# Attention and a gated expert layer on one core: pairs of column blocks in one bank for the first batch, and one head group's scores on four row strips

## The chip, the cores and the metric

The kernel runs on one core of one Trainium2 chip. The metric is the device time of one execution in microseconds, the median of several runs. Engines are named as in the profile: PE is TensorE (matmul), PEld its weight loads, DVE is VectorE, ACT is ScalarE, POOL is GpSimd, SP is SyncE. A lower time is better.

## The reference

Softmax attention over 8 batches of 12 heads, 448 tokens and 64 channels, and behind it a two-layer expert with a SiLU gate over all 3584 tokens.

```
scores = matmul(q, k^T) / 8;  attn = softmax(scores);  a = matmul(attn, v)
x = a with its heads side by side: 3584 x 768
h = x @ w_in            (768 x 2048)
g = h / (1 + exp(-h))
out = g @ w_out         (2048 x 768)
```

Inputs and the output are float32; the kernel computes in float16 with float32 sums.

## The kernel before

Work is cut into units of one batch and one head group (4 of the 12 heads). Batch 0 is cut in two pieces of 224 tokens (`PIECES`, line 211), so it has six units, 0 to 5; each later batch has three of 448 tokens. For a unit, `scores` (line 358) multiplies keys and queries. A head has 64 channels, held as two planes (`e`) of 32 rows, so a matmul uses one of four row strips of PE, one strip per head. The banks come in pairs: `y` = 0 holds heads 0 and 1, `y` = 1 heads 2 and 3, and there are two such pairs (`s_ring`). `expo` (line 378) takes the exponential of one pair of banks on ACT. `attend` (line 433) multiplies it, on four column strips, with ones (part 0, the sums) and with the values (parts 1 and 2). `inverse` (line 445) and `norm` (line 475) make x on DVE, and transposes on DVE (`turn_k`, `turn_q`) prepare keys and queries.

In `qk_seq` (lines 1289 to 1294) a unit below `HALVES` = 6, that is, every unit of batch 0, issues its scores in halves: one burst for `y` = 0 and one for `y` = 1, each on two row strips and each needing one free pair of banks. A unit from `HALVES` on issues one burst on all four strips and needs both pairs.

The first expert matmul, `ffn1` (line 503), goes by column blocks `f` of 128 of the 2048 columns, six matmuls each over the 768 rows. For batch 0 each of the two pieces has its own 16 blocks of 224 tokens; a bank holds 512 numbers per partition, and every block takes a bank of its own (tag `m`, four banks, shared with the attend tiles and the results of the second matmul). `tanh` (line 516) makes tanh(h) on ACT, with three buffers, and `gate` (line 547) computes (tanh(h) + 1) h on DVE, into `G`; x was made half as large, which turns this into the SiLU. The gate gives the bank back. `plain` (line 717) is the second matmul for the first four token tiles of batch 0, and `product` (line 701) for the later ones.

The order of every engine is laid down when the kernel is built. A planner (`Order`, line 82, and the loop at line 1473) keeps a clock for each engine with assumed durations, picks what PE does next among scores, attend tiles and expert work, and lets ACT and DVE take ready operations by their bias. What it emits is each engine's program; on the chip an engine runs it in order and waits at semaphores. So a small change of a duration or a ring moves many later instructions. Until the first block of `ffn1`, PE fills gaps with matmuls on zeros (`run_zeros`, line 1464), which hold one of the four `m` banks. The loads are issued by POOL in a fixed order; the results are stored from SP.

Names in the profile: `s` scores, `E` exponentials, `a` attend tiles, `xT` x, `h` first matmul, `th` Tanh, `G` gates, `o` and `p` second matmul, `T` sums of exponentials, `z` the zeros.

Of the kernel before, what the change touches and what calls it, by code (L numbers as in the profile page):

```python
# [9 lines left out]
FP16 = mybir.dt.float16  # L10
FP32 = mybir.dt.float32
AF = mybir.ActivationFunctionType
ALU = mybir.AluOpType
# [12 lines left out]
def mm(n):  # L26
    return n / 2400.0 + 0.0026


def act(n):  # L30
    return n * 0.00087 + 0.13
# [138 lines left out]
def kernel(  # L170
# [9 lines left out]
    nc = tc.nc  # L180
# [20 lines left out]
    LONES = (0, 1, 2, 3)  # L201
    NPL = 4
    EAGER = 1
    HALVES = 6
    NEAR, LATE = 0.15, -2.0
    COLD, FIRST = 8.5, 47
    SHY = 0.5
# [11 lines left out]
    sb = ctx.enter_context(tc.tile_pool(name="sb", bufs=1))  # L219
    ps = ctx.enter_context(tc.tile_pool(name="ps", bufs=1, space=bass.MemoryType.PSUM))  # L220
# [134 lines left out]
    def per_burst(n):  # L355
        return 2 if units[n][0] == 0 else 1
# [111 lines left out]
    def x3(b, cc):  # L468
        if (b, cc // 3) not in xT:
            xT[(b, cc // 3)] = sb.tile(  # L470
                [128, 3, S], FP16, name=f"xT_{b}_{cc // 3}", tag="xT", bufs=NX3
            )
        return xT[(b, cc // 3)]
# [15 lines left out]
    def times(out, w, x, start, stop, strips):  # L489
        cut = 32 if strips else 128  # L490
        for i in range(0, 128, cut):
            nc.tensor.matmul(  # L492
                out=out[i : i + cut],
                lhsT=w[:, i : i + cut],
                rhs=x,
                start=start,
                stop=stop,
                skip_group_check=True,
            )

    h_t, th_t, o_t = {}, {}, {}

    def ffn1(b, f, t0, t1, strips):
        h = ps.tile([128, 512], FP32, name=f"h_{b}_{f}_{t0}", tag="m", bufs=4)
        for cc in range(NDC):
            times(
                h[:, 0 : t1 - t0],
                w_in_t[:, cc, 128 * f : 128 * (f + 1)],
                x3(b, cc)[:, cc % 3, t0:t1],
                cc == 0,  # L510
                cc == NDC - 1,
                strips,
            )
        h_t[(b, f, t0)] = h

    def tanh(b, f, t0, t1):
        th = sb.tile([128, t1 - t0], FP16, name=f"th_{b}_{f}_{t0}", tag="th", bufs=3)
        nc.scalar.activation(out=th, in_=h_t[(b, f, t0)][:, 0 : t1 - t0], func=AF.Tanh)  # L518
        th_t[(b, f, t0)] = th


# [4 lines left out]
    G = const.tile([128, NFF, 2 * S], FP16, name="G")  # L526
# [20 lines left out]
    def gate(b, f, t0, t1):  # L547
        r = b % 2
        cut = 6 * 128 - S if b % 4 == 1 else S
        for lo, hi, dst, at in ((0, cut, G, S * r), (cut, S, X, -cut)):  # L550
            lo, hi = max(lo, t0), min(hi, t1)
            if lo < hi:
                nc.vector.scalar_tensor_tensor(  # L553
                    out=dst[:, f, at + lo : at + hi],
                    in0=th_t[(b, f, t0)][:, lo - t0 : hi - t0],
                    scalar=1.0,
                    in1=h_t[(b, f, t0)][:, lo - t0 : hi - t0],
                    op0=ALU.add,
                    op1=ALU.mult,
                )  # L560
# [223 lines left out]
    od = Order(SHY)  # L784
    s_ring, m_ring, e_ring = Ring(2), Ring(4), Ring(NE)
# [3 lines left out]
    kt_op, qt_op, exp_op, rdn_op, x_op, g_op = {}, {}, {}, {}, {}, {}  # L789
# [54 lines left out]
    for n in range(NB0 + NG, NU):  # L844
        b, hg = units[n][:2]
# [40 lines left out]
    moe = []  # L886
    x_left = {}
    ffn1_left = {b: 0 for b in range(B)}
# [5 lines left out]
    quads, gates_of = [], {}  # L894

    def queue_ffn1(b, g0, g1):
        t0, t1 = 32 * g0, 32 * g1
        for f in range(NFF) if b == 0 else [x for f in range(HF) for x in (f, f + HF)]:

            def run(f=f):  # L900
                strips = b > 0 and od.mode == "cols" and bool(qk_seq or av_seq)
                op = Op("PE", NDC * mm(t1 - t0), lambda: ffn1(b, f, t0, t1, strips), tail=PE_OUT)
                if warm["on"]:
                    warm["on"] = False
                    m_ring.give(od.now)
                m_ring.take()
                od.on_pe(op, "cols" if strips else "full")
                th = od.add(
                    Op("ACT", act(t1 - t0), lambda: tanh(b, f, t0, t1), [op], -3 if b == 0 else -0.3, tail=0.2)
                )  # L910
                g = Op(
                    "DVE",
                    (t1 - t0) / 960.0 + 0.13,
                    lambda: gate(b, f, t0, t1),
                    [th],
                    -4,
                    then=m_ring.give,
                )
                g_op.setdefault((b, f), []).append(od.add(g))
                ffn1_left[b] -= 1  # L920

            def deps(f=f):
                made = [(x_op[(b, cc, g0)], cc * mm(t1 - t0)) for cc in range(NDC)] + ld_win[f]

                u, r = divmod(b, 2)
                for qd in range(NT * B // 4) if u else ():
                    if any(t // NT == u - 1 and (r or t % NT < 4) for t in (2 * qd, 2 * qd + 1)):
                        made += (
                            [plain_op.get(x) for x in ((0, 0), (0, 1), (1, 0), (1, 1))]
                            if qd == 0  # L930
                            else [pr_op.get((qd, m)) for m in (1, 2, 3, 4, 7)]
                        )
                return made

            moe.append((deps, 1, run, ()))
            ffn1_left[b] += 1

    pair_w, pair_x = {}, {}
# [297 lines left out]
    def after_x(n):  # L1236

        b, hg, g0, g1 = units[n]
        x_left[(b, g0)] = x_left.get((b, g0), NG) - 1
        if x_left[(b, g0)]:  # L1240
            return
        if b == PB:
            return
        if b > PB:
            for qd in range(1, NT * B // 4):
                if max(batches(qd)) >= PB:
                    queue_quad(qd)
            return
        queue_ffn1(b, g0, g1)
        if g1 < TPP:  # L1250
            return
        if b == 0:
            sums_w((5, 6, 4))
            for j in range(2):
                for t in range(2):
                    queue_plain(t, j)
        for qd in range(1, NT * B // 4):
            if max(batches(qd)) == b:
                queue_quad(qd)
# [28 lines left out]
    for ns in jobs:  # L1288
        if len(ns) == 1:
            split = ((0,), (1,)) if ns[0] < HALVES else ((0, 1),)  # L1290
            qk_seq += [(ns, c, ys) for c in range(NCH // per_burst(ns[0])) for ys in split]
        else:
            split = ((0,), (1,)) if ns[0] < HALVES else ((0, 1),)
            qk_seq += [([n], c, ys) for n in ns for c in range(NCH - 1) for ys in split]
# [178 lines left out]
    while True:  # L1473
# [44 lines left out]
        if warm["on"] and od.free["PE"] <= od.now and wait > 0.06 and od.now > 0.9:  # L1518
            each = mm(128) if od.now > COLD else 0.107
            n = max(1, int((wait - 0.06) / each), int(wait / each + 0.9) * (od.now < COLD))  # L1520
            if warm.pop("first", None):
                n = FIRST
# [36 lines left out]
```

## Time and profile before

| What | Value |
|---|---|
| Median of three runs | 392.9 us (392.55 to 393.38) |
| The profiled execution's own time | 392.49 us |
| Its span in the profile | 390.7 us |
| Granted clock of PE | 90% of full speed or more in each of 40 slices |
| Tanh, 224 wide (batch 0) | 32 of 363 ns |
| Tanh, 448 wide | 80 of 545 ns |
| Gate, 224 wide (batch 0) | 32 of 382 ns |
| Gate, 448 wide | 48 of 616 ns |
| Exponential, 128 x 896 | 156 of 915 ns |
| Add of exponentials on DVE | 40 of 1084 ns |
| Block of `ffn1`, 6 matmuls of 224, ahead of another one | 0.575 us on PE |

The times come from the profiled execution. A busy time of PE is modelled at its ends, since matmuls overlap in the pipe: what a group costs PE is read as the distance from its start to the start of the next group. In a line of the timeline the columns are start, duration, engine, line of the kernel, operation, output and input, the tile's shape and the count; a bracket gives the engine's idle time before it and what ended that. "issue" means that the profile shows nothing that was waited for.

### The profile page before, as it was taken

The numbers are of one execution on the slowest core, as the hardware profiler recorded it, in microseconds if no ns is written. First come the engines' busy times: TensorE is split into PE (matmuls) and PEld (weight loads), VectorE is DVE, ScalarE is ACT, GpSimd is POOL, SyncE is SP. The second block draws the span as 40 slices with busy tenths as digits, with TensorE's granted clock in tenths as the row PEclk, the third lists the DMA queues.
The fourth block names the chain that finished last, engine by engine and source line by source line (L and its number), as shares of the span: only waits on it lengthen the run. The fifth ranks groups of instructions, "written<-read, shape, count | busy, mean of one in ns | idle before, by whom it ended". The sixth has DMA issues, their size and how long they took to land.

```text
span 390.7 us, 10672 instructions
## 1 busy us (share of the span) xinstructions
PE 384.3 (98%) x4369; PEld 206.3 (53%) x4369; DVE 274.6 (70%) x570; ACT 253.7 (65%) x399; POOL 89.1 (23%) x173
## 2 busy tenths in 40 slices
PE   8999999999999999999999999999999999999995
PEld 7667774444454444545445444544445655556663
DVE  2466676999996877987588758666869984447441
ACT  4988885697766779666774676466783238882220
POOL 7632365415006243400643014000000000000000
PEclk9999999999999999999999999999999999999999
DMA  7999999929039582814956139002100131001333
GB/s 114 202 210 210 159 161 190 187 42 139 1 62 151 121 105 40 119 47 89 145 82 88 40 73 168 7 0 59 27 0 3 42 93 29 0 3 41 92 95 98
DMA packets 35361, 34.52 MB, mean 88 GB/s; under 512 B 11376, under 2 KB 33776, under 8 KB 35312
## 3 DMA queue, kind: packets, MB, share of 16 engines
q0 software_dynamic: 24784, 22.82, 39.5%
q1 hardware_dynamic: 9952, 10.33, 9.8%
q8 instruction: 34, 0.56, 0.6%
q10 hardware_dynamic: 576, 0.69, 0.6%
q14 instruction: 15, 0.12, 0.1%
HBM read 45.61 MB, written 11.01 MB: 145 GB/s over the span
## 4 chain that ended last, share of the span: by engine, by line
PE 97%; DMA 1%; ACT 1%; issue 0%; POOL 0%; DVE 0%; POOLq 0%
PE p L492 31%; PE h L492 29%; PE s L346 13%; PE a L409 11%; PE f L492 8%; PE o L492 3%; PE a L425 2%; DMA rq<-in_q_dram 1%; PE z L1468 1%; ACT E L383 1%; POOL rk L255 0%; ACT ost L768 0%; DVE rq L333 0%; ACT th L518 0%; POOLq L1543 0%
## 5 line engine op out<-in xcount | busy, mean ns | idle before, releaser
L383 ACT ACTIVATE E<-s 128x896 f16<-128x896 f32 (+1 forms) x172 | 149.8, 915 | 38.0 <-PE s L346 36.5
L492 PE MATMUL h<-xT,w_in_t 128*32 128x448 f16 (+2 forms) x1086 | 117.2, 336 | 0.0
L492 PEld LDWEIGHTS <-w_in_t 128*128 128x128 f16 (+1 forms) x1158 | 71.2, 97 | 56.3 <-issue 11.5
L518 ACT ACTIVATE th<-h 128x448 f16<-128x448 f32 (+1 forms) x112 | 54.2, 493 | 36.8 <-PE h L492 31.1
L553 DVE SCALAR_TENSOR_TENSOR G<-th,h 128x448 f16<-128x448 f16 (+2 forms) x112 | 55.7, 509 | 23.4 <-ACT th L518 21.7
L492 PEld LDWEIGHTS <-G 128*128 128x128 f16 (+1 forms) x580 | 43.1, 98 | 32.4 <-issue 4.6
L768 ACT COPY ost<-p 128x384 f32<-128x384 f32 x52 | 24.9, 480 | 53.5 <-PE p L492 47.1
L346 PE MATMUL s<-rq,KT 32*128 32x448 f16 (+4 forms) x768 | 51.0, 337 | 0.8 <-ACT E L383 0.4
L280 POOL DMA_DIRECT2D V<-in_v_dram x88 | 48.3, 559 | 14.2 <-DMA w_out_t<-in_moe_w_out_dram 6.8
L492 PE MATMUL p<-w_out_t,G 128*128 128x384 f16 (+1 forms) x352 | 49.5, 326 | 0.0
L409 PE MATMUL a<-E,V 128*32 128x448 f16 (+2 forms) x864 | 42.3, 333 | 0.0
L492 PEld LDWEIGHTS <-S 128*128 128x128 f16 (+1 forms) x408 | 30.0, 98 | 22.7 <-issue 2.3
L261 POOL DMA_DIRECT2D rq<-in_q_dram x27 | 15.1, 558 | 102.6 <-PE s L346 79.0
L492 PE MATMUL p<-D,S 128*128 128x384 f16 (+1 forms) x256 | 37.2, 326 | 0.0
L774 DVE TENSOR_TENSOR ost<-p,ost 128x384 f32<-128x384 f32 x39 | 21.6, 554 | 18.7 <-PE p L492 14.9
L480 DVE SCALAR_TENSOR_TENSOR xT<-a,rdn 128x448 f16<-128x448 f32 (+1 forms) x54 | 30.4, 569 | 5.8 <-PE a L409 3.6
L346 PEld LDWEIGHTS <-KT 32*128 32x128 f16 (+2 forms) x864 | 17.5, 98 | 29.1 <-issue 27.3
L409 PEld LDWEIGHTS <-V 128*32 128x32 f16 (+1 forms) x864 | 20.5, 96 | 18.8 <-issue 7.6
L394 DVE TENSOR_TENSOR T<-E,E 128x1792 f16<-128x1792 f16 x20 | 21.7, 1084 | 8.0 <-ACT E L383 8.0
L394 DVE TENSOR_TENSOR T<-T,E 128x1792 f16<-128x1792 f16 x20 | 21.7, 1083 | 5.7 <-ACT E L383 5.7
L315 DVE STREAM_TRANSPOSE KT<-rk 128x256 f32<-128x256 f32 (+3 forms) x48 | 16.6, 385 | 6.7 <-DMA rk<-in_k_dram 5.9
L492 PE MATMUL p<-w_out_t,S 128*128 128x384 f16 (+1 forms) x152 | 19.1, 326 | 0.0
(67 smaller groups left out, 321.1 us busy)
## 6 DMA issues: line engine op xcount, KB each, us to landing
out_dram<-ost SPq DMA_DIRECT2D x194, 48.0 KB, 1.6
rk<-in_k_dram POOLq DMA_DIRECT2D x24, 224.0 KB, 5.8
rq<-in_q_dram POOLq DMA_DIRECT2D x21, 224.0 KB, 5.7
w_in_t<-in_moe_w_in_dram POOLq DMA_DIRECT2D x6, 512.0 KB, 11.2
w_out_t<-in_moe_w_out_dram POOLq DMA_DIRECT2D x4, 768.0 KB, 13.5
V<-in_v_dram POOLq DMA_DIRECT2D x43, 64.0 KB, 3.7
V<-in_v_dram POOLq DMA_DIRECT2D x40, 48.0 KB, 4.0
out_dram<-ost SPq DMA_DIRECT2D x8, 96.0 KB, 2.1
```

The source lines that it names most:

```text
L280: nc.gpsimd.dma_start(out=VT[b][32 * x : 32 * (x + 1), hs, 0:count, :], in_=v[b, hs].rearrange("h (i g) d -> i h g d", g=TPP)[:, :, first ...
L315: nc.vector.transpose(out=pairs[:, x:y, 0:count], in_=t[:, first : first + count * (y - x)].rearrange("p (x c) i -> p x c i", c=count),)
L346: nc.tensor.matmul(out=pS[p0 : p0 + 32 * (x1 - x0), h % 2, at : at + nq], lhsT=KT[(b, hg)][32 * h : 32 * (h + 1), c, x0:x1, :, e], rhs=QT[ ...
L383: nc.scalar.activation(out=E[(n, w)][0:kr, 2 * y : 2 * y + 2, 0:nk], in_=pS_t[(n, w, y)][0:kr, :, 0:nk], func=AF.Exp, scale=attn_scale,)
L394: nc.vector.tensor_tensor(out=T[n], in0=T[n] if step else E[(n, 0)], in1=E[(n, step + 1)], op=ALU.add,)
L409: nc.tensor.matmul(out=a[32 * h : 32 * (h + 1), 0:nq], lhsT=w, rhs=e[k0:k1, h, at : at + nq], start=start, stop=stop,)
L480: nc.vector.scalar_tensor_tensor(out=x3(b, cc)[:, cc % 3, 32 * g0 : 32 * g1], in0=acc[(n, part)][:, 0:nq], scalar=0.5, in1=rdn_t[n].rearra ...
L492: nc.tensor.matmul(out=out[i : i + cut], lhsT=w[:, i : i + cut], rhs=x, start=start, stop=stop, skip_group_check=True,)
L518: nc.scalar.activation(out=th, in_=h_t[(b, f, t0)][:, 0 : t1 - t0], func=AF.Tanh)
L553: nc.vector.scalar_tensor_tensor(out=dst[:, f, at + lo : at + hi], in0=th_t[(b, f, t0)][:, lo - t0 : hi - t0], scalar=1.0, in1=h_t[(b, f, ...
L768: nc.scalar.copy(out=ost(qd, *OUT[m]), in_=bank(qd, BANK[m]))
L774: nc.vector.tensor_tensor(out=t, in0=bank(qd, BANK[m]), in1=t, op=ALU.add)
```

## The change

Three edits, and what the planner makes of them.

First, batch 0's blocks of the first matmul go in pairs. `blocks(b)` is 2 for batch 0 and 1 for the others. Block `f` even opens a bank, block `f` + 1 writes the next 224 columns of the same bank. One Tanh and one gate of 448 serve both, the gate with a three-dimensional access that spreads the two blocks over `G`. The planner takes one bank for a pair, and Tanh and gate depend on the pair's second block. In batch 0 there are then 16 Tanh and 16 gates in place of 32 each.

Second, the wait of an odd block is tied to the even one before it, which has to have been issued (`parts`).

Third, `HALVES` is 5 in place of 6. Unit 5, the last head group of batch 0, issues its scores in two bursts of 16 matmuls on all four row strips in place of four bursts of 8.

```diff
-    HALVES = 6
+    HALVES = 5
...
     def ffn1(b, f, t0, t1, strips):
-        h = ps.tile([128, 512], FP32, name=f"h_{b}_{f}_{t0}", tag="m", bufs=4)
+        i = f % blocks(b)
+        if i == 0:
+            h_t[(b, f, t0)] = ps.tile(
+                [128, 512], FP32, name=f"h_{b}_{f}_{t0}", tag="m", bufs=4
+            )
+        h = h_t[(b, f - i, t0)]
         for cc in range(NDC):
             times(
-                h[:, 0 : t1 - t0],
+                h[:, (t1 - t0) * i : (t1 - t0) * (i + 1)],
...
+    def blocks(b):
+        return 2 if b == 0 else 1
+
     def tanh(b, f, t0, t1):
-        th = sb.tile([128, t1 - t0], FP16, name=f"th_{b}_{f}_{t0}", tag="th", bufs=3)
-        nc.scalar.activation(out=th, in_=h_t[(b, f, t0)][:, 0 : t1 - t0], func=AF.Tanh)
+        n = (t1 - t0) * blocks(b)
+        th = sb.tile([128, n], FP16, name=f"th_{b}_{f}_{t0}", tag="th", bufs=3)
+        nc.scalar.activation(out=th, in_=h_t[(b, f, t0)][:, 0:n], func=AF.Tanh)
...
-            if lo < hi:
+            if b == 0 and lo < hi:
+                nc.vector.scalar_tensor_tensor(
+                    out=G[:, f : f + 2, t0:t1],
+                    in0=th_t[(b, f, t0)].rearrange("p (f t) -> p f t", f=2),
+                    scalar=1.0,
+                    in1=h_t[(b, f, t0)][:, 0 : 2 * (t1 - t0)].rearrange("p (f t) -> p f t", f=2),
+                    op0=ALU.add,
+                    op1=ALU.mult,
+                )
+            elif lo < hi:
...
-                m_ring.take()
+                n = blocks(b)
+                if f % n == 0:
+                    m_ring.take()
                 od.on_pe(op, "cols" if strips else "full")
+                ffn1_left[b] -= 1
+                if f % n < n - 1:
+                    parts.append(f)
+                    return
...
             def deps(f=f):
+                if f % blocks(b) and f - 1 not in parts:
+                    return [None]
```

The built order of PE in the new kernel, from unit 3's sums on, where it leaves the old one: unit 3's attend (all three groups), unit 5's first burst, unit 4's sums, one zeros matmul, unit 4's attend, the first block of `ffn1`, unit 5's second burst, five more blocks, unit 6's first scores, unit 5's attend. The old order: unit 3's sums, one zeros matmul, then unit 5's four half bursts, each followed by one attend group (the last by two), the first block, unit 6's first scores, unit 5's attend. Behind that the two orders differ in detail until the second block of batch 4 and are then the same to the end. The work itself is the same, but that four matmuls of the second layer in batch 0 no longer run as four column strips each (12 instructions fewer).

More of the change, by code (lines that the diff above doesn't have):

```diff
@@ L513, in ffn1 @@
             )
-        h_t[(b, f, t0)] = h
+    def blocks(b):
+        return 2 if b == 0 else 1
     def tanh(b, f, t0, t1):
-        th = sb.tile([128, t1 - t0], FP16, name=f"th_{b}_{f}_{t0}", tag="th", bufs=3)
-        nc.scalar.activation(out=th, in_=h_t[(b, f, t0)][:, 0 : t1 - t0], func=AF.Tanh)
+        n = (t1 - t0) * blocks(b)
+        th = sb.tile([128, n], FP16, name=f"th_{b}_{f}_{t0}", tag="th", bufs=3)
+        nc.scalar.activation(out=th, in_=h_t[(b, f, t0)][:, 0:n], func=AF.Tanh)
         th_t[(b, f, t0)] = th
@@ L896, in queue_ffn1 @@
     def queue_ffn1(b, g0, g1):
-        t0, t1 = 32 * g0, 32 * g1
+        t0, t1, parts = 32 * g0, 32 * g1, []
         for f in range(NFF) if b == 0 else [x for f in range(HF) for x in (f, f + HF)]:
@@ L905, in run @@
                     m_ring.give(od.now)
-                m_ring.take()
+                n = blocks(b)
+                if f % n == 0:
+                    m_ring.take()
                 od.on_pe(op, "cols" if strips else "full")
+                ffn1_left[b] -= 1
+                if f % n < n - 1:
+                    parts.append(f)
+                    return
+                f0, nq = f - n + 1, n * (t1 - t0)
                 th = od.add(
-                    Op("ACT", act(t1 - t0), lambda: tanh(b, f, t0, t1), [op], -3 if b == 0 else -0.3, tail=0.2)
+                    Op("ACT", act(nq), lambda: tanh(b, f0, t0, t1), [op], -3 if b == 0 else -0.3, tail=0.2)
                 )
@@ L912, in run @@
                     "DVE",
-                    (t1 - t0) / 960.0 + 0.13,
-                    lambda: gate(b, f, t0, t1),
+                    nq / 960.0 + 0.13,
+                    lambda: gate(b, f0, t0, t1),
                     [th],
@@ L918, in run @@
                 )
-                g_op.setdefault((b, f), []).append(od.add(g))
-                ffn1_left[b] -= 1
+                od.add(g)
+                for i in range(f0, f + 1):
+                    g_op.setdefault((b, i), []).append(g)
             def deps(f=f):
+                if f % blocks(b) and f - 1 not in parts:
+                    return [None]
                 made = [(x_op[(b, cc, g0)], cc * mm(t1 - t0)) for cc in range(NDC)] + ld_win[f]
@@ L933, in deps @@
                 return made
-            moe.append((deps, 1, run, ()))
+            moe.append((deps, int(f % blocks(b) == 0), run, ()))
             ffn1_left[b] += 1
```

## The prediction

> **What bounds the kernel now.** I read the page first, for the engines and the chain, then the timeline of PE where the order of work changes, then the transfers of narrow windows. The page:
>
> ```profile
> PE 384.3 (98%) x4369; PEld 206.3 (53%) x4369; DVE 274.6 (70%) x570; ACT 253.7 (65%) x399; POOL 89.1 (23%) x173
> ...
> q8 instruction: 34, 0.56, 0.6%
> ...
> PE 97%; DMA 1%; ACT 1%; issue 0%; POOL 0%; DVE 0%; POOLq 0%
> ```
>
> PE is busy for 98% of the span and is 97% of the chain, so an edit counts only by what it does to PE: work taken off it, changes of tiling mode, or stalls. ACT and DVE have slack on the average (65% and 70%). The second line is the queue that fetches instructions: 0.56 MB in 34 packets is 16.5 KB each, and PE's 8738 instructions over 34 are 257 per packet. I come back to it. PE's timeline, the start and the stretch in which the order changes:
>
> ```profile
> 5.97 0.60 PE L346 MATMUL s<-rq,KT 32*128 32x224 f16 x16 [0.33 <-DVE rq L333]
> 6.50 0.62 PE L1468 MATMUL z<-zeros 128*128 128x128 f16 x8
> ...
> 24.11 0.57 PE L409 MATMUL a<-E,ones 128*32 128x224 f16 x16
> 24.61 0.23 PE L1468 MATMUL z<-zeros 128*128 128x128 f16 x1
> 24.78 0.57 PE L346 MATMUL s<-rq,KT 32*128 32x224 f16 x8
> 25.28 0.57 PE L409 MATMUL a<-E,V 128*32 128x224 f16 x16
> 25.78 0.57 PE L346 MATMUL s<-rq,KT 32*128 32x224 f16 x8
> 26.28 0.57 PE L409 MATMUL a<-E,V 128*32 128x224 f16 x16
> 26.78 0.60 PE L346 MATMUL s<-rq,KT 32*96 32x224 f16 x8
> 27.31 0.56 PE L409 MATMUL a<-E,ones 128*32 128x224 f16 x13
> 28.13 0.28 PE L409 MATMUL a<-E,ones 96*32 96x224 f16 x3 [0.26 <-issue]
> 28.34 0.60 PE L346 MATMUL s<-rq,KT 32*96 32x224 f16 x8
> 28.87 0.96 PE L409 MATMUL a<-E,V 128*32 128x224 f16 x32
> 29.76 0.75 PE L492 MATMUL h<-xT,w_in_t 128*128 128x224 f16 x6
> ```
>
> The price of a group is the distance between two starts. PE runs in a fixed order without holes except one: the group at 27.31 stops after 13 of its 16 matmuls and goes on at 28.13. It took 1.03 where its like at 25.28 took 0.50, and the profile names no semaphore for the 0.53. The other hole after 10 us is here:
>
> ```profile
> 50.85 1.27 DVE L553 SCALAR_TENSOR_TENSOR G<-th,h 128x224 f16<-128x224 f16 x4
> 51.28 1.70 PE L409 MATMUL a<-E,V 128*32 128x448 f16 x32
> 51.58 1.72 ACT L383 ACTIVATE E<-s 128x896 f16<-128x896 f32 x2
> 52.91 1.00 PE L346 MATMUL s<-rq,KT 32*128 32x448 f16 x8
> 53.85 3.05 PE L492 MATMUL h<-xT,w_in_t 128*128 128x224 f16 x30
> ```
>
> The gates came late behind an add of 1.05 us on DVE at 49.88. So the attend group got its bank 0.08 us late (51.28), one Tanh waited for its buffer, the two exponentials behind it ended at 53.30, and the scores at 52.91, which need both of their banks, took 0.94 instead of 0.51.
>
> **The change part by part.** PE's order is the same in both kernels up to the group at 24.11 and again from the second block of batch 4 (241.4 us) to the end. So the sum is made over what lies between.
>
> *Scores of unit 5.* Four bursts of 8 matmuls on two row strips become two of 16 on four. Now: 0.50 + 0.50 + 0.53 + 0.53 = 2.06 us (24.78 to 25.28, 25.78 to 26.28, 26.78 to 27.31, 28.34 to 28.87). No row has the interleaved form. Upper end: strips do not overlap, 2.06 again. Lower end: as many columns per strip as the 448-wide burst at 30.44, which ends at 30.94: 0.50, and 0.53 with 96 rows, 1.03. Nearest is the kernel's first burst, 16 matmuls from 5.97 to 6.50, 0.53 with its strips one pair behind the other; with 0.03 for 96 rows I take 0.53 + 0.56 = 1.09. Gain 0.97.
>
> *Mode changes.* Two attend groups in a row take 0.89 (28.87 to 29.76), 0.40 and 0.49, against 0.50 ahead of scores. In the new order the first two of unit 3 stand ahead of another attend group: 0.2 saved. The second burst of unit 5 now stands between two blocks of the first matmul, which costs one more change, 0.1. Gain 0.1.
>
> *Pairs in a bank.* 32 Tanh of 363 ns become 16 of 545 (the 448-wide row), 32 gates of 382 ns become 16 of 616: 11.6 to 8.7 us on ACT and 12.2 to 9.9 on DVE, both under PE, so nothing by itself. PE's matmuls are the same. What it can cost is that a bank is held from the first block's start to the pair's gate. A pair takes 2 x 0.575 on PE, and Tanh and gate behind it some 1.4 with hops; four banks last 4.6 us. Following each bank by its rows to the first block of batch 1, I find every one free 0.4 us or more before PE asks. Bounds for what is not followed behind that: 0 to 0.5 us lost; I take 0, because PE had no hole over 0.1 us from 54 to 380 us with such work.
>
> *The wait at 52.91.* In the new order a block of the first matmul (0.67) stands between the attend groups and these scores, and the Tanh three pairs on waits for a gate that is done before the add on DVE starts. PE comes 2.8 us behind the previous burst, its exponentials end some 2.5 behind it. Gain 0.08 + 0.43 = 0.51; bounds 0 and 0.51.
>
> *Moved steps.* The full burst waits for both exponentials of unit 4 (end 25.14; PE comes at 25.41) and the second one for both of unit 5's first (end about 28.0); behind them stand attend groups and first blocks. The first block of the first matmul goes ahead of the second burst; its weights have landed by 23.0 us, the second half's by 33.9 (first used at about 36.6), the last quarter of w_out by 61.2 (used at about 65). The turn of the next keys moves behind unit 4's norms, ending near 30.8; its scores come at 33.1. POOL's and SP's queues keep their order.
>
> *The hole at 28.13.* Windows of the transfers show one fetch packet at 19.6, 25.7 and 31.7 each, six microseconds apart in the stretch where q0 keeps the engines over 100% busy, the middle one being
>
> ```profile
> q8 instruction: 1, 0.02, 5.1%
> ```
>
> between 25.6 and 26.7, and none from 26.7 to 31.6. PE passes some 257 instructions in the same six microseconds. My reading: PE came to the end of a block and the next, landed at 26.6, was usable 1.5 us later. At the other two boundaries PE comes 1.5 to 1.6 us behind the landing too. The block holds the same instructions by number in the new kernel: 86 matmuls after 24.11, which is now the sixth of unit 4's second attend group. PE gets there at 24.11 + 0.40 + 0.40 + 0.50 + 0.53 + 0.49 + 0.16 + 0.10 = 26.69. The packet was asked for before 24.11, so it comes at the same time: PE stands until 28.13, 1.44 us instead of 0.53. Loss 0.91. The next block would be usable near 34.1, and PE asks for it at about 34.6. Bounds: gain 0.53 (no hole) to loss 0.91.
>
> [...]
>
> Sum: -0.97 - 0.10 - 0.51 + 0.91 = -0.67 us. The profiled execution took 392.49 us around its span of 390.7, 0.4 under the median of 392.9; the span goes to 390.0 and the median to 392.2.
>
> **Rivals.** *The hole is no block boundary.* Then it is gone or as short as before: -0.97 - 0.10 - 0.51 - 0.53 = -2.11, 390.8 us. For it: PE passes the boundaries before and behind with no hole. Against: it stands where packet and count put it. [...]
>
> *Banks held too long (slower).* Where attend tiles of 0.87 us take one of the four banks, three are left, 3.45 us. A pair whose Tanh finds an exponential ahead (0.92) and whose gate finds an add (1.08) holds its bank for 1.15 + 0.2 + 0.92 + 0.55 + 1.08 + 0.62 = 4.5 us. PE then stands about 1 us, and the place comes at three points in batch 0 (unit 5's attend, unit 6's sums, unit 6's attend). It decides once two of them meet both: 392.2 + 2 = 394.2. For it: DVE's add did this once before, at 49.88. Against: two Tanh and two gates less stand in each queue, and the order puts the add elsewhere.
>
> *The burst gains nothing.* If strips interleave no better than in turn, 0.97 stays: 393.2. Against it the row at 5.97.
>
> **How the numbers follow.** Forecast 62%, no-boundary 18%, held banks 12%, burst without gain 8%. What a measurement can tell from no change is about 0.2%, 0.79 us. The forecast's gain of 0.67 lies just under it; with 0.4 us of doubt on the unfollowed stretch and the runs (their spread is 0.8) it is faster in 25, the same in 36, slower in 1 of its 62. No-boundary is faster; the burst case splits 1, 6, 1; held banks slower. Faster 0.44, the same 0.42, slower 0.14. The range 390.5 to 393.4 holds the first two and the burst case, and leaves out mainly held banks.
>
> **What would show it.** In the new profile: two bursts of 16 at about 25.4 and 29.6, each near 0.55; a hole in unit 4's second attend group that ends near 28.1, with a fetch packet near 25.7; no hole at unit 8's first scores; Tanh near 545 and gates near 616 ns, 16 each; the second block of batch 4 at about 240.7. Wrong would be: no hole at 26.7 (the first rival), PE waiting for G in batch 0 (the second), bursts near 1 us (the third), or new holes from 75 to 240 us.

## The result and the profile after

| | Before | After |
|---|---|---|
| Median, side by side | 392.74 us (392.12 to 393.38, 10 runs) | 391.52 us (391.33 to 392.24, 10 runs) |
| Ratio | | 0.9973, 95% interval 0.9965 to 0.9981 |
| The profiled execution | 392.49 us, span 390.7 | 391.46 us, span 389.7 |

The change is worth 1.2 us in these medians and 1.0 us in the two spans; the forecast was 0.67. A second set of runs gave 391.85 beside 392.51 us, a ratio of 0.9981 (0.9972 to 0.9990): 0.7 us. So the runs alone give the gain no closer than 0.7 to 1.2 us. The page of the kernel after: the engines, PE's share of the chain, and the groups of Tanh and of gates.

```profile
PE 382.6 (98%) x4357; PEld 205.2 (53%) x4357; DVE 273.7 (70%) x554; ACT 251.9 (65%) x383; POOL 89.1 (23%) x173
...
PE 97%; DMA 1%; issue 0%; ACT 0%; POOL 0%; DVE 0%; POOLq 0%
...
L526 ACT ACTIVATE th<-h 128x448 f16<-128x448 f32 x96 | 52.4, 546 | 33.5 <-PE h L492 27.8
```

PE still sets the end. The Tanh have one width left, 546 ns, and 1.8 us of ACT and 0.9 us of DVE went without PE's share changing. The gates by shape show the 16 new ones at 618 ns beside the old 448-wide ones at 616:

```profile
L570 DVE SCALAR_TENSOR_TENSOR G<-th,h 128x448 f16<-128x448 f16 x48 | 29.1, 616 | 14.7 <-ACT th L526 13.8
L561 DVE SCALAR_TENSOR_TENSOR G<-th,h 128x448 f16<-128x448 f16 x16 | 9.9, 618 | 8.1 <-ACT th L526 8.1
```

PE's timeline of the kernel after where the order changed, and at unit 8's first scores:

```profile
24.17 0.57 PE L409 MATMUL a<-E,ones 128*32 128x224 f16 x16
24.56 0.95 PE L409 MATMUL a<-E,V 128*32 128x224 f16 x32
25.44 0.58 PE L346 MATMUL s<-rq,KT 32*128 32x224 f16 x16
25.95 0.57 PE L409 MATMUL a<-E,ones 128*32 128x224 f16 x16
26.45 0.23 PE L1495 MATMUL z<-zeros 128*128 128x128 f16 x1
26.61 0.36 PE L409 MATMUL a<-E,V 128*32 128x224 f16 x5
27.84 0.86 PE L409 MATMUL a<-E,V 128*32 128x224 f16 x27 [0.86 <-issue]
28.63 0.75 PE L492 MATMUL h<-xT,w_in_t 128*128 128x224 f16 x6
29.31 0.61 PE L346 MATMUL s<-rq,KT 32*96 32x224 f16 x16
29.85 3.05 PE L492 MATMUL h<-xT,w_in_t 128*128 128x224 f16 x30
...
51.86 1.71 PE L409 MATMUL a<-E,V 128*32 128x448 f16 x32
53.49 0.75 PE L492 MATMUL h<-xT,w_in_t 128*128 128x224 f16 x6
54.18 0.57 PE L346 MATMUL s<-rq,KT 32*128 32x448 f16 x8
54.68 1.51 PE L492 MATMUL h<-xT,w_in_t 128*128 128x224 f16 x14
```

Read by starts: the two bursts of unit 5 take 0.51 (25.44 to 25.95) and 0.54 (29.31 to 29.85). The hole stands in unit 4's second attend group: five matmuls, then nothing until 27.84, with no semaphore named. The two groups take 2.02 us (26.61 to 28.63) against 0.89 for the pair ahead of the same block in the kernel before (28.87 to 29.76), so PE stood 1.13 us; before, it stood 0.53 (a group of 1.03 for one of 0.50). Unit 8's first scores take 0.50 in place of 0.94.

Where the time went, added up over all starts of PE from unit 3's sums to the second block of batch 4:

```
               before   after   difference
scores          34.78   33.22   -1.56
attend          37.26   37.65   +0.39
first matmul    77.30   77.40   +0.10
second matmul   67.74   67.75   +0.01
zeros            0.16    0.16    0
sum            217.24  216.18   -1.06
```

The second block of batch 4 starts at 240.35 in place of 241.35, and PE ends 1.01 us earlier: what was won by then stays.

### The profile page after: what moved, and what is told of

It reads as the page before. It is cut to its first block, busy times and chain, and to the rows that moved or that the text cites. A ratio compares the mean times of both kernels' runs of the same rounds, so it can differ in the third digit from the quotient of the medians.

```text
span 389.7 us, 10594 instructions
## 1 busy us (share of the span) xinstructions
PE 382.6 (98%) x4357; PEld 205.2 (53%) x4357; DVE 273.7 (70%) x554; ACT 251.9 (65%) x383; POOL 89.1 (23%) x173
## 4 chain that ended last, share of the span: by engine, by line
PE 97%; DMA 1%; issue 0%; ACT 0%; POOL 0%; DVE 0%; POOLq 0%
PE p L492 31%; PE h L492 29%; PE s L346 13%; PE a L409 11%; PE f L492 8%; PE o L492 3%; PE a L425 2%; DMA rq<-in_q_dram 1%; PE z L1495 1%; ACT E L383 0%; POOL rk L255 0%; ACT ost L785 0%; DVE rq L333 0%; POOLq L1570 0%
## 5 line engine op out<-in xcount | busy, mean ns | idle before, releaser
L526 ACT ACTIVATE th<-h 128x448 f16<-128x448 f32 x96 | 52.4, 546 | 33.5 <-PE h L492 27.8
L570 DVE SCALAR_TENSOR_TENSOR G<-th,h 128x448 f16<-128x448 f16 (+1 forms) x80 | 44.3, 560 | 18.3 <-ACT th L526 16.8
L346 PE MATMUL s<-rq,KT 32*128 32x448 f16 (+4 forms) x768 | 49.4, 337 | 0.9 <-DVE rq L333 0.5
L346 PEld LDWEIGHTS <-KT 32*128 32x128 f16 (+2 forms) x864 | 16.7, 98 | 28.7 <-issue 26.5
L409 PEld LDWEIGHTS <-V 128*32 128x32 f16 (+1 forms) x864 | 20.4, 96 | 19.9 <-issue 7.9
L492 PE MATMUL p<-D,G 128*128 128x384 f16 (+1 forms) x128 | 19.1, 326 | 0.0
```

The lines of the kernel that those rows point to most:

```text
L346: nc.tensor.matmul(out=pS[p0 : p0 + 32 * (x1 - x0), h % 2, at : at + nq], lhsT=KT[(b, hg)][32 * h : 32 * (h + 1), c, x0:x1, :, e], rhs=QT[ ...
L409: nc.tensor.matmul(out=a[32 * h : 32 * (h + 1), 0:nq], lhsT=w, rhs=e[k0:k1, h, at : at + nq], start=start, stop=stop,)
L492: nc.tensor.matmul(out=out[i : i + cut], lhsT=w[:, i : i + cut], rhs=x, start=start, stop=stop, skip_group_check=True,)
L526: nc.scalar.activation(out=th, in_=h_t[(b, f, t0)][:, 0:n], func=AF.Tanh)
L570: nc.vector.scalar_tensor_tensor(out=dst[:, f, at + lo : at + hi], in0=th_t[(b, f, t0)][:, lo - t0 : hi - t0], scalar=1.0, in1=h_t[(b, f, ...
```

## Experiments

Theories. *Blocks*: the forecast's sum, with the hole at the end of a block of 256 instructions (128 matmuls with their weight loads) whose successor is late because its fetch waits behind the loads. *Rivals*: the hole belongs to that matmul or its data, or the gain comes from the pairs and not from the scores. Matmuls are counted from 0 in PE's stream; by count the hole is at matmul 476 in both kernels (28.13 us before, 27.84 after), and by blocks of 128 matmuls the ends before it would be at 348 and 220.

**One edit at a time.** The kernel before with the scores' edit alone, and the kernel after without it:

```diff
 (on the kernel before)
-    HALVES = 6
+    HALVES = 5
 (on the kernel after)
-    HALVES = 5
+    HALVES = 6
```

> The kernel before with the scores of unit 5 in two bursts alone (blocks of the first matmul stay one to a bank). My sum: scores -1.0 us, mode changes -0.1; the instruction at which PE stood (matmul 476 of its stream, counted from 0) is here the sixth of unit 4's second attend group, as in the kernel after, so the hole grows from 0.6 to about 1.1: +0.5. That is -0.6 us against before, and up to -1.1 if the late scores of unit 8 come on time as well. Rival, the gain comes from pairs in a bank: no change, within 0.2 us of before.

> The kernel after with the scores of unit 5 in four bursts again, so pairs in a bank alone. My sum: scores, mode changes and the hole at matmul 476 (here again in unit 4's sums, as before, 0.6 us) as in the kernel before; what is left is the wait at unit 8's first scores: -0.5 us if the pairs remove it, 0 if they do not. Rival, the gain comes from pairs in a bank: -1.2 us, as much as the whole change.

> The kernel before with the scores of unit 5 in two bursts alone, looked at once more, for its trace. By my sum it is 0.6 us faster than before and by the earlier run no faster. If the sum up to 34 us holds (scores -1.0, mode changes -0.1, hole +0.5), the gain is there at unit 6's first scores and is given back behind, by waits of PE for banks or for gates, 0.6 us together.

Against before in the same sets (392.57 us), pairs alone: 392.20 us, ratio 0.9992 (0.9983 to 1.0001). Over the stretch of the sum above they take 216.67 us, 0.57 less than before, of which 0.53 is scores: the wait at unit 8's first scores is gone (53.12 to 53.63 in that trace, 0.51), and the hole is as before, 0.49. That is the first branch of what was expected; the rival's 1.2 us did not come.

The scores' edit alone was no faster: 392.60 us, ratio 1.0 (0.9991 to 1.0008), against the 0.6 us forecast for it. PE's timeline of this kernel, from a second run of it (392.30 us):

```profile
25.38 0.58 PE L346 MATMUL s<-rq,KT 32*128 32x224 f16 x16
25.89 0.57 PE L409 MATMUL a<-E,ones 128*32 128x224 f16 x16
...
26.55 0.37 PE L409 MATMUL a<-E,V 128*32 128x224 f16 x5
28.04 0.86 PE L409 MATMUL a<-E,V 128*32 128x224 f16 x27 [1.12 <-issue]
28.82 0.75 PE L492 MATMUL h<-xT,w_in_t 128*128 128x224 f16 x6
29.50 0.60 PE L346 MATMUL s<-rq,KT 32*96 32x224 f16 x16
```

The bursts take 0.51 and 0.54 here too (the second to 30.04), and unit 8's first scores take 0.51 (53.29 to 53.80 in this trace): the wait there goes with this edit alone as well. But PE stood 2.27 - 0.89 = 1.38 us at matmul 476, 0.85 more than before, not the 0.5 that I had expected. By these terms the gain is 1.01 + 0.10 + 0.51 - 0.85 = 0.77 us, and the trace has 0.17 over the stretch. So 0.60 were lost behind 34 us, as I had written: 0.25 in a burst of scores at 71.9 us (0.75 for 0.50), 0.15 in an attend group at 209.5 us (2.54 for 2.39), and 0.2 in small differences that the order makes. The hole took 0.35 more than I had put there, and the gain at unit 8's first scores made up for it. The two edits do not add up: -0.17 and -0.57 apart, -1.06 together. Either alone removes the wait at unit 8's first scores, so together it counts once; against that, the hole comes out at 1.13 with both and at 1.38 with the scores' edit alone, and the losses at 71.9 and 209.5 us are not in the kernel after.

**Is it the place in the stream?** More warm-up matmuls at the start move every later instruction along, with the planner's order and the work unchanged. The first of two runs has 57, the second has `n, m, w = 108, 32, 52` in the same line:

```diff
             warm["z"] = ps.tile([128, 512], FP32, name="z", tag="m", bufs=4)
+            n, m, w = 57, 128, 106
+        else:
+            m, w = 128, 128
         for _ in range(n):
             nc.tensor.matmul(
-                out=warm["z"][:, 0:128], lhsT=zeros, rhs=zeros, start=True, stop=True
+                out=warm["z"][0:m, 0:w], lhsT=zeros[:, 0:m], rhs=zeros[:, 0:w], start=True, stop=True
             )
```

> The kernel after with 57 warm-up matmuls of 106 columns in place of the first 47 of 128, so that every later matmul stands ten places further on in PE's stream while the order and the work stay. If PE stands at the end of a block of instructions, the hole stays at matmul 476, which is now the fourteenth or so of unit 4's sums (the first attend group of unit 4), ten matmuls earlier in the work, about 0.4 us earlier, and it lasts 1.2 to 1.5 us; the time is 0 to 0.4 us over after. Rival, the hole belongs to that matmul or to what it reads: it stays at the sixth matmul of the second attend group, 1.1 us, and the time is that of after.

> The kernel after with 108 narrow warm-up matmuls (32 columns of weights, 52 columns) in place of the first 47, so that every later matmul stands 61 places further on. By the blocks, their ends now fall at the scores of unit 3 (about 20 us), in unit 3's second attend group (about 24.8 us) and in the fifth block of the first matmul (about 30 us); following the fetch times of the kernel after, which take 5.3 to 5.9 us from one end of a block until the next block is usable, PE stands 0.2 to 0.8 us in unit 3's attend group and not in unit 4's: the time is 0.3 to 0.9 us below after. Rival, the hole belongs to that matmul: it stays there at 1.1 us and the time is that of after.

With 57, PE's timeline is

```profile
26.27 0.47 PE L409 MATMUL a<-E,ones 128*32 128x224 f16 x12
28.25 0.28 PE L409 MATMUL a<-E,ones 96*32 96x224 f16 x4 [1.50 <-issue]
28.46 0.23 PE L1498 MATMUL z<-zeros 128*128 128x128 f16 x1
28.62 0.96 PE L409 MATMUL a<-E,V 128*32 128x224 f16 x32
```

The hole moved into unit 4's sums, at their thirteenth matmul, which is again number 476 of the stream; the second attend group, where it had been, runs through. It lasted 2.19 - 0.50 = 1.69 us, more than the 1.2 to 1.5 expected. PE also stood 0.2 us at the block's end before, matmul 348 (22.13; that burst of scores took 0.71 for 0.50), 1.38 us behind the end of its packet. The median was 392.20 us beside 392.57 before, ratio 0.9996 (0.9985 to 1.0007): no gain that the runs tell from none, where the kernel after had 1.2 and 0.7 us in its two sets. (The trace is of an execution of 393.89 us, and its granted clock is 0.59 from 29.5 to 32 us; only what stands ahead of that is read here.) The rival that the matmul itself or its data is late has fallen.

With 108, the same stretch has no hole (matmul 476 is now in unit 3's second attend group, at 25.01):

```profile
24.81 0.95 PE L409 MATMUL a<-E,V 128*32 128x224 f16 x32
25.69 0.58 PE L346 MATMUL s<-rq,KT 32*128 32x224 f16 x16
26.20 0.57 PE L409 MATMUL a<-E,ones 128*32 128x224 f16 x16
26.70 0.23 PE L1498 MATMUL z<-zeros 128*128 128x128 f16 x1
26.86 0.96 PE L409 MATMUL a<-E,V 128*32 128x224 f16 x32
27.75 0.75 PE L492 MATMUL h<-xT,w_in_t 128*128 128x224 f16 x6
```

What is left is 0.2 us at matmul 604, in the blocks of the first matmul (30.91); the 0.2 to 0.8 us that I expected at 476 did not come. The median is 390.83 us, ratio to before 0.9955 (0.9943 to 0.9967).

**The worth of the change without the hole.** The kernel before with the same 108 warm-up matmuls:

> The kernel before with the 108 narrow warm-up matmuls of the earlier run, nothing else. The ends of the blocks fall 61 matmuls earlier in the work; by the fetch times of the kernel after, 5.3 to 5.9 us, PE stands 0 to 0.3 us at each of two places in place of 0.5 at one: 0 to 0.5 us below before. With the 390.8 us of the kernel after with the same warm-up, that gives the worth of the change without the hole: by my sum 1.6 us (scores 1.0, mode changes 0.1, the wait at unit 8's scores 0.5). Rival, the warm-up itself gave the gain: 1.7 us below before, as there.

392.27 us beside 392.52, ratio 0.9996 (0.9987 to 1.0005): not told from no change by the runs, while its trace shows the hole gone (unit 4's sums take 0.50, from 27.35 to 27.85) and the wait at unit 8's first scores still there:

```profile
50.85 1.70 PE L409 MATMUL a<-E,V 128*32 128x448 f16 x32
52.48 1.00 PE L346 MATMUL s<-rq,KT 32*128 32x448 f16 x8
53.42 2.76 PE L492 MATMUL h<-xT,w_in_t 128*128 128x224 f16 x27
```

With the hole at 476 out of both kernels the change is worth 392.27 - 390.83 = 1.44 us by the medians (of two sets, whose kernels before differ by 0.05) and 216.81 - 215.32 = 1.49 us over the stretch, with the 0.2 us at matmul 604 still in the second; my sum without the hole is 0.97 + 0.10 + 0.51 = 1.58. So the warm-up did not bring the gain by itself, and the change's own three gains hold.

**Is the fetch late because of the loads?** Two tests. The first measures blocks by themselves, in a kernel of matmuls only:

```diff
+NA, NB, NC = 768, 768, 640
...
+    run(NA, ones, 224)
+    nc.gpsimd.memset(ones, 1.0)
...
+    run(NB, half, 224)
+    run(NC, half, 448)
```

The `memset` writes the ones again, so POOL waits there until the matmuls that read them are done (23.4 us, put down to PE in the profile); the loads of w_in, w_out and k, left out here, follow it.

> A stream of matmuls alone, without the kernel's work: 768 of 224 columns on four column strips with no loads running, then 768 more of these and 640 of 448 columns while the loads of w_in, w_out and k run on POOL's queue; the output is a copy of one bank. By the blocks: 128 matmuls of 224 columns take 3.2 us at 25 ns each. With no loads no hole over 0.2 us; with loads a hole of 2.1 to 2.7 us at every 128th matmul, since a block then takes 5.3 to 5.9 us; with 448 columns (48 ns, 6.1 us to a block) no hole over 0.3 us. [...]

Its timeline, first without loads and then with them:

```profile
11.82 3.25 PE L207 MATMUL a<-E,ones 128*32 128x224 f16 x128 [0.48 <-issue]
15.55 3.25 PE L207 MATMUL a<-E,ones 128*32 128x224 f16 x128 [0.48 <-issue]
19.28 3.25 PE L207 MATMUL a<-E,ones 128*32 128x224 f16 x128 [0.48 <-issue]
...
26.46 3.25 PE L207 MATMUL a<-E,half 128*32 128x224 f16 x128 [0.48 <-issue]
33.76 4.91 PE L207 MATMUL a<-E,half 128*32 128x224 f16 x128 [4.04 <-issue]
39.95 3.25 PE L207 MATMUL a<-E,half 128*32 128x224 f16 x128 [1.28 <-issue]
45.87 4.58 PE L207 MATMUL a<-E,half 128*32 128x224 f16 x128 [2.67 <-issue]
51.79 3.25 PE L207 MATMUL a<-E,half 128*32 128x224 f16 x128 [1.35 <-issue]
57.72 12.54 PE L207 MATMUL a<-E,half 128*32 128x224 f16 x241 [2.67 <-issue]
```

Every line but the last is one block: 128 matmuls, then a hole with no semaphore. Without loads a block takes 3.73 us (11.82 to 15.55 to 19.28; one took 3.45) for 3.0 us of matmuls; I had expected no hole there. The first block after the loads began took 7.3 us (26.46 to 33.76), the next 6.2. From then on a block takes 5.9 us (39.95, 45.87, 51.79, 57.72), whether its matmuls took 4.6 us, with a granted clock of 0.66 from 45 to 50 us, or 3.2, with 1.00 from 40 to 45. The 448-wide matmuls take 6.05 us to a block, and PE passes the ends of their blocks with no stop. So in this stream a block had a time of its own, and PE stood for what its matmuls left of it. The loads added to that time ahead of the packet: the next block's packet starts 1.1 to 1.2 us behind a block's first matmul without loads and 3.6 to 3.8 with them (4.8 in the first), and lasts 0.9 to 1.3 us in both.

The ten ends of blocks at which PE stood in a row are 128 matmuls apart, each with one weight load (2176 of both in the page): 256 instructions, where the page of the kernel before has 257 to a packet.

The second test holds back, in the kernel after, w_in's second half and all loads behind it until unit 2's sums are done:

```diff
...
+            def emit():
+                if f0 and c == 0:
+                    nc.gpsimd.memset(ones, 1.0)
+                load_w_in(c, f0, f1)
+
+            emit.late = LATER if f0 else 0.0
...
+    LATER = 22.0
```

> The kernel after with the loads of w_in's second half, and all loads behind them on POOL's queue, held until unit 2's sums are done (about 21.7 us), so that the load queue runs dry for a moment at about 23 us, when the fetch of the block that is late in the kernel after is waiting. If the fetch is late because the loads stand ahead of it: its packet starts at 22.3 to 24 us in place of 25.5, the hole at matmul 476 goes from 1.1 us to 0.1 or less, and the time is 1.0 us below after, less what the later loads cost (w_in's second half lands about 1.3 us later; the first block that reads it would wait 0 to 0.5 us). Rival, the block takes its time whatever the loads do: the packet stays near 25.5, the hole stays, and the time is that of after or above.

The loads went out from 22.16 us on, but the traffic fell only from 24 us on, so the pause came a little late: 160 and 134 GB/s in the windows from 24 to 26 us, where the kernel after moved 210 and 223. The packet started 2.48 us behind matmul 348 in place of 3.29, and PE stood 0.28 us at matmul 476 (27.14 to 28.31 for the pair). A new hole of 0.34 came at matmul 348, whose packet was 0.6 us later than in the kernel after; why, this run does not show. The sum of the two holes is 0.62 us in place of 1.13, and the median 391.03 us beside 392.52 (ratio 0.9961, 0.9948 to 0.9973). With the pause the packet came earlier and the hole shrank, which the rival did not allow; but packets came as early without a pause in the runs where matmul 348 started at 19.8 to 19.9 us (the table below), so it is the stream of matmuls alone that shows what the loads do. The full 1.0 us was not reached, and a pause at the right moment was not tried.

**A version that is faster than both.** 56 more warm-up matmuls, 24 of them at the start and the others by two narrow ones for each later one, beside the kernel after on the same chip:

```diff
+            n, m, w = 71, 128, 77
+        elif n > 1:
+            n, m, w = 2 * n, 32, 64
+        else:
+            m, w = 128, 128
```

> The kernel after once more, on the chip and beside the runs of the next kernel, for a comparison of the two: 391.5 us, hole at matmul 476 of 1.0 to 1.2 us.

> The kernel after with 56 more warm-up matmuls: 71 of 77 columns in place of the first 47, and two of 64 columns (32 columns of weights) for every later one but the single ones. The ends of the blocks fall 56 matmuls earlier in the work. With 61 more, PE stood 0.3 us at matmul 604 and its first scores ran 0.2 us late; with 56 that block is asked for 0.1 us later and used 0.4 us later, so no hole is left over 0.1 us from 18 to 40 us, and the first scores come as in the kernel after: 0.9 to 1.2 us below after, 390.3 to 390.6. Rival, narrow warm-up matmuls keep PE slow at the start or take longer than those they replace: 390.8 or more.

After: 391.85 us. In the trace of this set the granted clock is 0.54 from 33 to 40.4 us, PE took 7.5 us from matmul 348 (33.01) to 476 (40.49) and did not stand there, so the hole of 1.0 to 1.2 us was not read a second time. The new one: 390.70 us, ratio to before 0.9951 (0.9938 to 0.9963), 1.1 us below after. The first scores come at 5.90 (6.03 in the kernel after), and matmul 604 waits for nothing. But a hole of 0.42 is back at 476, and the total misses the 390.3 to 390.6 expected. What the fetches did in these kernels, from the packets of the instruction queue and PE's starts (us; one trace of each kernel is read, so how far a hole varies between executions of one kernel is not shown):

```
                      matmul 348   packet          matmul 476   stood there
before                22.17        25.71 - 26.60   28.13        0.53
after                 22.22        25.51 - 26.40   27.84        1.13
scores' edit alone    22.14        25.75 - 26.64   28.04        1.38
pairs alone           22.57        26.15 - 27.04   28.51        0.49
57 warm-up            22.13        25.82 - 26.71   28.25        1.69
108 warm-up           19.82        22.33 - 23.22   25.01        0
71 and doubled        19.93        22.78 - 23.67   25.30        0.42
```

Wherever PE stood at matmul 476, it went on 1.40 to 1.63 us behind the packet's end. Where matmul 348 started at 22.1 to 22.6 us, the packet started 3.3 to 3.7 us behind it; where it started at 19.8 to 19.9, 2.5 to 2.9, and why it is less there no run here shows. These few tenths and the time at which PE arrives (27.6 us before, 26.7 after) decide the hole's size. With 108 warm-up matmuls PE came to 476 5.2 us behind 348, where the kernel after took 4.5: the work in that block is longer, and its packet was early.

## Why the prediction was right

- *Scores of unit 5.* 0.53 + 0.56 forecast, 0.51 + 0.54 measured; gain 1.01 for 0.97. The row of the first burst was the right one to go by, and the rival of a burst without gain is out.
- *Mode changes.* Unit 3's three groups start at 24.17, 24.56 and 24.95, and the burst at 25.44: 0.39, 0.39 and 0.49, as forecast; the block of the first matmul ahead of the second burst takes 0.68 (28.63 to 29.31) for 0.575, the 0.1 of the sum.
- *Pairs in a bank.* Tanh 546 and gates 618 ns for 545 and 616. ACT and DVE were busy 1.8 and 0.9 us less, not the 2.9 and 2.3 that counts times means gave; under PE, busy 98% in both pages, it made no difference. From 18 to 385 us no matmul of PE started late by 0.25 us or more but at the hole: no bank was held too long, and that rival, the slower side, did not come near.
- *The wait at unit 8's first scores.* Gone, 0.44 of the 0.51 in the scores themselves. It goes with either edit alone and stays where only the stream is shifted, so what removes it is the planner's new order, as the prediction had it: PE then comes 2.8 us or more behind the burst before (51.35 to 54.18 in the kernel after, 50.48 to 53.29 with the scores' edit, 49.91 to 53.12 with the pairs), and 2.2 where the wait stands (50.69 to 52.91 in the kernel before).
- *The hole.* The place was right to the matmul, and PE arrived at 26.7 as forecast. The step that was mis-sized is "The packet was asked for before 24.11, so it comes at the same time: PE stands until 28.13". When a packet is asked for no run shows; this one started 3.29 us behind matmul 348, where it was 3.54 before. It came 0.20 us earlier (25.51) and PE went on 1.44 us behind its end instead of 1.53, at 27.84: a loss of 1.13 - 0.53 = 0.60 in place of 0.91. With the scores' edit alone the same place lost 0.85. My number is thus within what one kernel differs from the next; the error was to carry a packet's time over without an allowance.
- *The sum.* -1.01 - 0.10 - 0.51 + 0.60 = -1.02 us, against -1.06 over the stretch and -1.0 in the spans; forecast -0.67. The 0.66 us of the second set of runs agrees with it by chance: the terms come to 1.0. The first rival (no boundary, 390.8 us) is refuted as a reason by the shifted streams, although a stream that was shifted far enough has just that time.

## What to carry to other kernels

Where PE runs short matmuls while loads run, count matmuls from one fetch packet to the next, and compare the time that 256 instructions take with the 5.9 us (3.7 without loads) that a block took here in the stream of matmuls alone. The change made such a stretch denser and paid part of its gain back at the block's end, 0.60 of 1.62 us; the scores' edit by itself lost 0.85 at the block's end and 0.6 further on, and gave nothing. If a hole names no semaphore and keeps its number in the stream, a few dozen more instructions in idle time ahead of it may move the block's end to where the work is longer, as 61 and 56 did here; ten more left it in nearly the same work, and PE stood longer there (1.69 us).

## What was not expected of the hardware

- Even with no load running, a block of 256 instructions took 3.73 us, so that a stream of matmuls of 24 ns each stood 0.7 us at the ends of four blocks of five, and 0.5 at the other.
- The time of a block did not add to that of its matmuls, it ran beside it: 5.9 us with loads for 3.2 us of work and for 4.6 us alike.
- With the 108 warm-up matmuls of 32 columns of weights ahead, the first eight scores of the kernel after took 0.33 us for 0.20 (6.06 to 6.39), and unit 3's sums came 0.24 us later. The kernel before with the same 108 took 0.25 (5.92 to 6.17), and its unit 3 came no later (24.11), so the narrow weights alone do not explain it. It stays open.
